# Attention, mixture of experts and gated layer in one kernel: who makes the low parts of the first expert's weights, and when the token list is turned

## The chip, the cores and the metric

The kernel runs on one core of a Trainium2 chip, as a single program with one launch. The metric is the device time in microseconds. The engines are called as in the profile: PE is TensorE, DVE is VectorE, ACT is ScalarE, POOL is GpSimd and SP is SyncE.

## What is computed

Three layers follow one another. Attention with a decay runs over 4 batches of 8 heads, 576 positions, 64 values a head. Its output is read as x with 2304 tokens of 512 values, and goes through a mixture of 8 experts in which each token uses one:

```python
logits = x @ w_gate
e_idx = np.argmax(logits, axis=1)
...
eom = 1.0 / (1.0 + np.exp(-(x @ w_output_gate)))
...
for e in range(E):
    mask = e_idx == e
    ...
    h = np.maximum(x[mask] @ w1[e], 0.0)
    ye = h @ w2[e]
    out[mask] = gate_w[mask, None] * eom[mask, e, None] * ye
```

with w1 of 512 x 1024 and w2 of 1024 x 512 for each expert. The third layer multiplies by w_in (512 x 2048), applies P(h) / (Q(h) + 1e-6) with a cubic P and a quadratic Q, and multiplies by w_out (2048 x 512).

## The kernel before

**Matmuls in two parts.** Operands of the experts and of the third layer are split in two: a high part (ScalarE copies the number into TensorE's float32r form) and a low part (the number less its high part). A product is three matmuls: high by high, high by low, low by high (`mm3`, lines 1164 to 1169, the second of the three on line 1168). `split_unit` (line 1054) does this for a unit of weights: a unit is a quarter of an expert (units 0 and 1 are the halves of w1, 2 and 3 those of w2), 128 x 2048 numbers. Line 1058 makes the high part, in two instructions on ScalarE, and line 1060 the low part, in two instructions on the engine that `on` names. `raw[u]` is the loaded unit, `wu[u]` the split one.

**Slots.** Tokens are sorted by expert into slots of 128. The pipelined loop runs over NPIPE = 22 slots; up to three more, if an expert distribution needs them, are done behind it under `tc.If(spill > 0)`. A small table `esl` describes each slot: whether its expert is a new one, which expert comes next, whether there is one, whether the slot is used. Fourteen small VectorE instructions on 25 partitions make it from `send0` and `pcol` (lines 1016 to 1030), right behind `ids`, the list of tokens of each slot (line 1007). `weights(u, s)` reads `esl`: on ScalarE and VectorE, to split a new expert's unit in slot s under a condition, and on SyncE, to load the next expert's unit into `raw[u]` (line 1110). `spill` is read from `esl` on all engines ahead of the loop (line 1263).

**The order inside a slot is written out by hand** (`tc.manual_schedule`): each engine takes its instructions in the order of the program. For slot s: `gather(s + 3)` (GpSimd, an indirect transfer of 128 rows of x, line 1142); `mm1(s, 0)` with unit 0; `trans_x(s + 1)` (four turns on TensorE, line 1161; then `hi_lo`: the high copy on ScalarE, line 1086, the low part on VectorE, line 1087, into `colA`); `weights(0, s + 1)`; `mm2(s - 1, 0)` and `trans_h(s, 0)` (turns of h, line 1182); `weights(2, s)`; `mm1(s, 1)` with unit 1; `weights(1, s + 1)`; `mm2(s - 1, 1)` and `trans_h(s, 1)`. Slot 0 has no earlier slot: it does `mm1(0,0)`, `trans_x(1)`, `mm1(0,1)`, `trans_h(0,0)`; its `trans_h(0,1)` and first `mm2` stand in slot 1, behind `trans_x(2)`.

**Pieces.** Between these stand four calls `pieces(2)` a slot. Each does two steps of `decode`, which turns w_in and w_out from 64-bit to 32-bit numbers: a transfer issued by GpSimd (line 1201), then ScalarE's absolute value `da` (line 1206) with VectorE's line 1207; line 1209; line 1211; line 1214; ScalarE's high copy (line 1219); VectorE's low part (line 1221).

**What is special in the first slots.** The low part of unit 0 is made ahead of the loop by VectorE, that of unit 1 by VectorE behind `trans_x(0)`, those of units 2 and 3 by GpSimd in slot 0. At slot 0's end stands `slot_tokens()` (line 1126): VectorE copies `ids` to numbers (line 1130), TensorE turns them (line 1132), VectorE copies them back (line 1133) and SyncE stores them as `sid_d`. At slot 1's end stands `dense_rows()` (lines 1112 to 1124), five VectorE instructions that make `yrow`. From slot 2 on, one `gather_word` a slot (line 1148) reads `sid_d` at `yrow`; there are 18.

Of the kernel before, what the change touches and what calls it, by code (L numbers as in the profile page):

```python
# [9 lines left out]
F32 = mybir.dt.float32  # L10
# [3 lines left out]
I32 = mybir.dt.int32  # L14
U32 = mybir.dt.uint32
AF = mybir.ActivationFunctionType
ALU = mybir.AluOpType
AX = mybir.AxisListType
# [3 lines left out]
P = 128  # L22
# [109 lines left out]
def tile_attention_moe_mlp(  # L132
# [16 lines left out]
    nc = tc.nc  # L149
# [3 lines left out]
    NT, DM = out.shape  # L153
    NE, _, FF = w1.shape
# [5 lines left out]
    NSLOT = (NT + NE * (P - 1)) // P  # L160

    NPIPE = min(NSLOT, NT // P + NE // 2)
# [9 lines left out]
    const = ctx.enter_context(tc.tile_pool(name="const", bufs=1))  # L172
# [41 lines left out]
    with ExitStack() as actx, ExitStack() as rctx:  # L214
# [666 lines left out]
        def t_(shape, dt=F32, name=None):  # L881
            return wk.tile(shape, dt, name=name, tag=name, bufs=1)
# [4 lines left out]
        def iota(shape, pattern, base, per_row, name, pool=None):  # L887
            t = pool.tile(shape, F32, name=name) if pool else t_(shape, name=name)
            nc.gpsimd.iota(
                t, pattern=pattern, base=base, channel_multiplier=per_row, allow_small_or_imprecise_dtypes=True  # L890
            )
            return t
# [2 lines left out]
        s1 = t_([P, NSLOT], F16, name="s1")  # L895
        nc.vector.tensor_copy(s1, iota([P, NSLOT], [[1, NSLOT]], 0, 0, "s1f"))
        row = iota([P, P], [[1, P]], 0, 0, "row")
        pcol = iota([P, 1], [[0, 1]], 0, 1, "pcol")

        tokv = iota([P, B, NI], [[S, B], [P, NI]], -(NT // 2), 1, "tokv").rearrange("p b i -> p (b i)")  # L900
        off = t_([P, B, NI], name="off")
# [33 lines left out]
            rows_copy(i)  # L935
        incl, pos3 = t_(SH, name="incl"), t_(SH, name="pos3")
        cnt, nsl = t_([P, NE], name="cnt"), t_([P, NE], name="nsl")
        send0 = t_([P, NE + 1], name="send0")
        nc.gpsimd.memset(send0, 0.0)
        send = send0[:, 1:]  # L940
        base = const.tile([P, NE], F32, name="base")
# [65 lines left out]
        nc.vector.tensor_scalar_add(ids, pid[:, :NSLOT], float(NT // 2))  # L1007

        q = slice(0, NSLOT)
        eq, eo = t_([P, NE + 1], name="eq"), t_([P, NE], name="eo")
        ee, en = t_([P, 1], name="ee"), t_([P, 1], name="en")
        esl = const.tile([P, 4], I32, name="esl")
        chg, usd = t_([P, 1], name="chg"), t_([P, 1], name="usd")
        nc.vector.tensor_scalar(eq[q], send0[q], pcol[q], None, op0=ALU.is_equal)
        nc.vector.tensor_reduce(chg[q], eq[q], AX.X, ALU.max)
        nc.vector.tensor_scalar(eo[q], send[q], pcol[q], None, op0=ALU.is_le)
        nc.vector.tensor_reduce(ee[q], eo[q], AX.X, ALU.add)
        nc.vector.tensor_single_scalar(usd[q], ee[q], NE - 0.5, ALU.is_lt)  # L1020

        nc.vector.scalar_tensor_tensor(eo[q], eo[q], 1.0e6, send[q], ALU.mult, ALU.add)
        nc.vector.tensor_reduce(en[q], eo[q], AX.X, ALU.min)
        nc.vector.tensor_scalar(eo[q], send[q], en[q], None, op0=ALU.is_le)
        nc.vector.tensor_reduce(en[q], eo[q], AX.X, ALU.add)
        nc.vector.tensor_tensor(chg[q], chg[q], usd[q], ALU.mult)
        nc.vector.tensor_copy(esl[q, 0:1], chg[q])
        nc.vector.tensor_scalar_min(esl[q, 1:2], en[q], NE - 1.0)
        nc.vector.scalar_tensor_tensor(esl[q, 2:3], en[q], NE - 0.5, chg[q], ALU.is_lt, ALU.mult)
        nc.vector.tensor_copy(esl[q, 3:4], usd[q])  # L1030


    wu_p = ctx.enter_context(tc.tile_pool(name="wu", bufs=1, reuse_waits="tile"))

    wu = [wu_p.tile([P, 2, KD, 512], F32R, name=f"wu{u}") for u in range(4)]
# [15 lines left out]
            in_offset=bass.IndirectOffsetOnAxis(ap=yrow[:, t : t + 1], axis=0),  # L1051
        )

    def split_unit(u, hi=True, lo=True, on=nc.vector):
        for c in (0, 2):
            w, r = wu[u][:, :, c : c + 2], raw[u][:, c : c + 2]
            if hi:
                nc.scalar.activation(w[:, 0], r, AF.Copy)  # L1058
            if lo:
                on.tensor_tensor(w[:, 1], r, w[:, 0].bitcast(F32), ALU.subtract)  # L1060


    for u in range(4):
        split_unit(u, lo=(u == 0))
    nc.scalar.activation(babs, coef[:, 4:6], AF.Abs)

    with ExitStack() as ectx:
        mk = ectx.enter_context(tc.tile_pool(name="mk", bufs=2, reuse_waits="tile"))
# [7 lines left out]
        def col_of(k):  # L1076
            return tuple(x[:, k] for x in colA)
# [12 lines left out]
        def weights(u, s):  # L1090

            if s:
                if s not in flags:
                    flags[s] = nc.values_load(
                        esl[s : s + 1, 0 : 1], engines=[mybir.EngineType.Activation, mybir.EngineType.DVE],
                        min_val=0, max_val=1,
                    )
                with tc.If(flags[s] > 0):  # L1098
                    split_unit(u)
            if u == order0:  # L1100
                nxt[s] = (
                    nc.sync.value_load(esl[s : s + 1, 1 : 2], min_val=0, max_val=NE - 1),
                    nc.sync.value_load(esl[s : s + 1, 2 : 3], min_val=0, max_val=1),
                )
            e, more = nxt[s]
            if u < 2:
                src = w1[bass.ds(e, 1), :, u * 512 : (u + 1) * 512].rearrange("o (c p) n -> p (o c) n", p=P)
            else:
                src = w2[bass.ds(e, 1), (u - 2) * 512 : (u - 1) * 512, :].rearrange("o (c p) n -> p (o c) n", p=P)
            nc.sync.dma_start(out=raw[u], in_=src, cond=more > 0, bounds_check="skip_entire_dma")  # L1110

        def dense_rows():

            dpad = const.tile([P, NE - 1], F32, name="dpad")
            nc.vector.tensor_tensor(dpad, base[:, 1:], base[:, : NE - 1], ALU.subtract)
            SD = [P, NTILE, NE - 1]
            past = const.tile(SD, F32, name="past")
            nc.vector.tensor_tensor(
                past, dns.unsqueeze(2).to_broadcast(SD), cume[:, 1:NE].unsqueeze(1).to_broadcast(SD), ALU.is_ge
            )  # L1120
            nc.vector.tensor_tensor(past, past, dpad.unsqueeze(1).to_broadcast(SD), ALU.mult)
            drow = const.tile([P, NTILE], F32, name="drow")
            nc.vector.tensor_reduce(drow, past, AX.X, ALU.add)
            nc.vector.tensor_tensor(yrow, drow, dns, ALU.add)

        def slot_tokens():

# [12 lines left out]
        def gather(s):  # L1140
            xg[s] = mk.tile([P, DM], F32, tag="xg", name="xg", bufs=3)
            nc.gpsimd.indirect_dma_start(
                out=xg[s], out_offset=None, in_=x_d[:, :],
                in_offset=bass.IndirectOffsetOnAxis(ap=ids[:, s : s + 1], axis=0),
            )
# [6 lines left out]
        def gather_y(k):  # L1152

            xg[NPIPE + k] = mk.tile([P, DM], F32, tag="xg", name="xg", bufs=3)
            rows_of(k, xg[NPIPE + k])

        def trans_x(s, to):
            pt = ps_x.tile([P, 512], F32, tag="px", name="px")
            t = xg.pop(s)
            for c in range(KD):  # L1160
                nc.tensor.transpose(pt[:, c * P : (c + 1) * P], t[:, c * P : (c + 1) * P], identf)
            xT[s] = hi_lo(pt, to)
# [93 lines left out]
        warm(10)  # L1256
        for s in range(3):
            gather(s)
        trans_x(0, col_of(0))
        weights(0, 0)  # L1260
        split_unit(1, hi=False)
        weights(1, 0)
        spill = nc.values_load(esl[NPIPE : NPIPE + 1, 3 : 4], min_val=0, max_val=1)
        words = deque(range(NTILE))
        for s in range(NPIPE):
            if s + 3 < NPIPE:
                gather(s + 3)
            else:
                gather_y(s + 3 - NPIPE)
            if s >= 2 and words:  # L1270
                t = words.popleft()
                gather_word(dtok[:, t : t + 1], sid_d[:, :], yrow[:, t : t + 1])
            mm1(s, 0)
            if s + 1 < NPIPE:
                trans_x(s + 1, col_of((s + 1) % 2))
                weights(0, s + 1)
            pieces(2)
            if s == 1:
                trans_h(0, 1, col_of(3))
                weights(3, 0)  # L1280
            if s:
                mm2(s - 1, 0)
                trans_h(s, 0, col_of(2))
            if s == 0:
                split_unit(2, hi=False, on=nc.gpsimd)
            weights(2, s)
            pieces(2)
            mm1(s, 1)
            if s + 1 < NPIPE:
                weights(1, s + 1)  # L1290
            pieces(2)

            if s:
                mm2(s - 1, 1)
                trans_h(s, 1, col_of(3))
                weights(3, s)
            else:
                trans_h(0, 0, col_of(2))
                split_unit(3, hi=False, on=nc.gpsimd)
            pieces(2)  # L1300
            if s == 0:
                slot_tokens()
            if s == 1:
                dense_rows()

        gather_y(3)
        for k in range(4):
# [3 lines left out]
        while words:  # L1311
            t = words.popleft()
# [193 lines left out]
```

## Time and profile before

| what | us |
|---|---|
| median of 3 runs | 952.83 (952.47 to 953.22) |
| the profiled execution, its time | 949.95 |
| the profiled execution, its span | 948.1 |
| PE busy | 894.9 |
| DVE busy | 755.4 |
| ACT busy | 623.7 |
| POOL busy | 347.2 |

The busy times are of the whole span, in which attention, experts and third layer follow one another; they are averages over stages with different limits. Times in the rows below count from the span's start. The attention part ends, and the slots begin, at about 240 us.

### The profile page before, as it was taken

The page shows a single profiled execution, that of the slowest core. Times are in us where ns is not written, and L with a number is a line of the kernel's source. Part 1 is how long each engine was busy: PE and PEld are TensorE (multiplying, and loading weights), DVE is VectorE, ACT ScalarE, POOL GpSimd, SP SyncE. Part 2 cuts the span into 40 slices and gives each one's busy share as a digit, 9 for nine tenths or more (in the row PEclk, how much of TensorE's full clock was granted, in tenths as well). Part 3 has the DMA queues.
Part 4 walks back from the last instruction along what each step waited for, and adds up shares of the span by engine and source line. Part 5 has one row for each costly group of instructions (what it writes and reads, how often), then busy time and mean ns, then how long its engine had stood idle before and what let it go on. Part 6 is the DMA issues. An engine that isn't in the chain of part 4 may idle for free. (4 is left out here: it accounts for less than half of the span.)

```text
span 948.1 us, 14923 instructions
## 1 busy us (share of the span) xinstructions
PE 894.9 (94%) x4732; PEld 713.5 (75%) x4733; DVE 755.4 (80%) x1410; ACT 623.7 (66%) x1274; POOL 347.2 (37%) x357
## 2 busy tenths in 40 slices
PE   5999999995589999999999999999999999999996
PEld 5665666563368888888888778889988889988885
DVE  6778888877948668978785499989989878889873
ACT  3787777777036456756653487887777677777664
POOL 7766565624612221312331123243332324223223
PEclk8999999998789999999999999999999999999999
DMA  6754546702455537878864312100100001000001
GB/s 171 168 150 131 157 127 207 210 15 99 138 208 189 194 114 273 298 257 285 287 228 145 135 57 67 34 27 30 34 34 12 23 1 45 24 1 34 1 0 45
DMA packets 50148, 110.26 MB, mean 116 GB/s; under 512 B 8405, under 2 KB 12526, under 8 KB 50062
## 3 DMA queue, kind: packets, MB, share of 16 engines
q1 hardware_dynamic: 39214, 74.09, 25.6%
q0 software_dynamic: 10848, 35.14, 10.8%
q8 instruction: 39, 0.64, 0.3%
q14 instruction: 47, 0.39, 0.1%
HBM read 151.79 MB, written 20.35 MB: 182 GB/s over the span
## 5 line engine op out<-in xcount | busy, mean ns | idle before, releaser
L1405 POOL TENSOR_TENSOR gl<-raw,gh 128x512 fp32r<-128x512 f32 (+1 forms) x80 | 95.4, 1194 | 243.4 <-ACT gh L1404 151.1
L1421 PE MATMUL pa<-wu,gl 128*128 128x512 f32 x288 | 113.0, 392 | 1.1 <-POOL gl L1405 1.1
L1419 PE MATMUL pa<-wu,gh 128*128 128x512 f32 x288 | 113.7, 395 | 0.0
L1420 PE MATMUL pa<-wu,gh 128*128 128x512 f32 x288 | 112.6, 391 | 0.0
L1384 ACT ACTIVATE raw<-ph 128x512 f32<-128x512 f32 (+1 forms) x80 | 44.3, 553 | 79.9 <-PE ph L1376 76.7
L496 ACT ACTIVATE pr<-t,mn 128x384 f32<-128x384 f32 (+3 forms) x128 | 71.1, 557 | 27.6 <-DVE mn L466 25.8
L1087 DVE TENSOR_TENSOR colAl<-px,colAh 128x512 fp32r<-128x512 f32 x70 | 48.0, 687 | 51.4 <-ACTq L1098 28.4
L1060 DVE TENSOR_TENSOR wu<-raw,wu 128x1024 fp32r<-128x1024 f32 x60 | 81.0, 1391 | 7.5 <-ACT wu L1058 7.3
L1387 DVE SCALAR_TENSOR_TENSOR raw<-raw,babs 128x512 f32<-128x512 f32 (+1 forms) x80 | 60.8, 760 | 24.2 <-ACT raw L1385 23.9
L1397 DVE SCALAR_TENSOR_TENSOR raw<-raw,coef,raw 128x512 f32<-128x512 f32 (+1 forms) x80 | 65.9, 824 | 17.6 <-ACT raw L1393 14.5
L1168 PE MATMUL ph<-wu,colAh 128*128 128x512 f32 x176 | 70.7, 402 | 8.2 <-DVE wu L1060 8.2
L1374 PE MATMUL ph<-colAh,wi 128*128 128x512 f32 x192 | 74.9, 390 | 0.8 <-ACTq L1315 0.8
L1375 PE MATMUL ph<-colAl,wi 128*128 128x512 f32 x192 | 74.8, 390 | 0.2 <-DVEq L1315 0.2
L1167 PE MATMUL ph<-wu,colAh 128*128 128x512 f32 x176 | 74.2, 421 | 0.7 <-ACT colAh L1086 0.7
L1376 PE MATMUL ph<-colAh,wi 128*128 128x512 f32 x192 | 74.7, 389 | 0.0
L466 DVE CUSTOM_DVE_ANT_0 t<-s,mask 128x384 f32<-128x384 f32 (+3 forms) x128 | 60.3, 485 | 16.9 <-ACT ot L280 6.9
L1169 PE MATMUL ph<-wu,colAl 128*128 128x512 f32 x176 | 70.7, 402 | 0.0
L1167 PE MATMUL py<-wu,colAh 128*128 128x512 f32 x176 | 70.5, 400 | 0.0
L1169 PE MATMUL py<-wu,colAl 128*128 128x512 f32 x176 | 68.8, 391 | 0.0
L1168 PE MATMUL py<-wu,colAh 128*128 128x512 f32 x176 | 68.7, 390 | 0.0
L614 PE MATMUL po<-pT,v 128*64 128x320 f32 (+4 forms) x448 | 66.4, 380 | 0.4 <-DVE pT L282 0.4
L1086 ACT ACTIVATE colAh<-px 128x512 fp32r<-128x512 f32 x70 | 41.6, 596 | 38.2 <-PE px L1182 25.2
(236 smaller groups left out, 2456.4 us busy)
## 6 DMA issues: line engine op xcount, KB each, us to landing
raw<-in_w_dram SPq DMA_DIRECT2D x92, 1024.0 KB
rk<-in_kT_dram SPq DMA_DIRECT2D x30, 288.0 KB
rq<-in_qT_dram SPq DMA_DIRECT2D x30, 288.0 KB
d<-in_w_in_dram POOLq DMA_DIRECT2D x16, 512.0 KB
d<-in_w_out_dram POOLq DMA_DIRECT2D x16, 512.0 KB
y_d<-ys SPq DMA_DIRECT2D x22, 256.0 KB
v<-in_v_dram SPq DMA_DIRECT2D x16, 256.0 KB
wo_d<-d SPq DMA_DIRECT2D x16, 256.0 KB
```

Of the source, the lines that this page charges most:

```text
L496: nc.scalar.activation(u["pr"][:, :w], u["t"][:, :w], AF.Exp, bias=u["mn"][:, 0:1], scale=-1.0, accum_out=sm[:, i, 2 * hp + h : 2 * hp + h ...
L1060: on.tensor_tensor(w[:, 1], r, w[:, 0].bitcast(F32), ALU.subtract)
L1167: nc.tensor.matmul(ps, hi[:, c, :], w[:, 0, c, :], start=start and c == 0, stop=False)
L1168: nc.tensor.matmul(ps, hi[:, c, :], w[:, 1, c, :], start=False, stop=False)
L1169: nc.tensor.matmul(ps, lo[:, c, :], w[:, 0, c, :], start=False, stop=stop and c == KD - 1)
L1374: nc.tensor.matmul(out_, wh, hi[:, :, c], start=(c == 0), stop=False)
L1375: nc.tensor.matmul(out_, wh, lo[:, :, c], start=False, stop=False)
L1376: nc.tensor.matmul(out_, wl_, hi[:, :, c], start=False, stop=(c == KD - 1))
L1405: nc.gpsimd.tensor_tensor(d["gl"], d["u_"], d["gh"].bitcast(F32), ALU.subtract)
L1419: nc.tensor.matmul(a_, gh[:, sl], wh, start=(m == 0), stop=False)
L1420: nc.tensor.matmul(a_, gh[:, sl], wl_, start=False, stop=False)
L1421: nc.tensor.matmul(a_, gl[:, sl], wh, start=False, stop=(m == MF - 1))
```

## The change

The low parts of all four units of the first expert are made by VectorE: those of units 0 and 1 one after the other behind the first three gathers are issued, those of units 2 and 3 at the places in slot 0 where GpSimd made them. The description of the slots becomes a function, `slot_info()`, with the same fourteen instructions, called behind `trans_x(0)`; its small tiles lie in a buffer of the tag `ys`, and `pcol` and `send0` move to the pool of constants. `slot_tokens()` moves from slot 0's end to slot 1's, ahead of `dense_rows()`; the words are gathered from slot 3 on; `spill` is read at slot 2's end.

```diff
-        pcol = iota([P, 1], [[0, 1]], 0, 1, "pcol")
+        pcol = iota([P, 1], [[0, 1]], 0, 1, "pcol", const)
...
-        send0 = t_([P, NE + 1], name="send0")
+        send0 = const.tile([P, NE + 1], F32, name="send0")
...
-        q = slice(0, NSLOT)
-        eq, eo = t_([P, NE + 1], name="eq"), t_([P, NE], name="eo")
-        ee, en = t_([P, 1], name="ee"), t_([P, 1], name="en")
-        esl = const.tile([P, 4], I32, name="esl")
-        chg, usd = t_([P, 1], name="chg"), t_([P, 1], name="usd")
-        nc.vector.tensor_scalar(eq[q], send0[q], pcol[q], None, op0=ALU.is_equal)
...
-        nc.vector.tensor_copy(esl[q, 3:4], usd[q])
...
-    def split_unit(u, hi=True, lo=True, on=nc.vector):
+    def split_unit(u, hi=True, lo=True):
...
-                on.tensor_tensor(w[:, 1], r, w[:, 0].bitcast(F32), ALU.subtract)
+                nc.vector.tensor_tensor(w[:, 1], r, w[:, 0].bitcast(F32), ALU.subtract)
...
     for u in range(4):
-        split_unit(u, lo=(u == 0))
+        split_unit(u, lo=False)
...
+        esl = const.tile([P, 4], I32, name="esl")
+
+        def slot_info():
+
+
+            q = slice(0, NSLOT)
+            t = mk.tile([P, DM], F32, tag="ys", name="info")
+            eq, eo, rest = t[:, 0 : NE + 1], t[:, 32 : 32 + NE], t[:, 64:68]
+            ee, en, chg, usd = (rest[:, k : k + 1] for k in range(4))
+            nc.vector.tensor_scalar(eq[q], send0[q], pcol[q], None, op0=ALU.is_equal)
+            nc.vector.tensor_reduce(chg[q], eq[q], AX.X, ALU.max)
+            nc.vector.tensor_scalar(eo[q], send[q], pcol[q], None, op0=ALU.is_le)
+            nc.vector.tensor_reduce(ee[q], eo[q], AX.X, ALU.add)
+            nc.vector.tensor_single_scalar(usd[q], ee[q], NE - 0.5, ALU.is_lt)
+
+            nc.vector.scalar_tensor_tensor(eo[q], eo[q], 1.0e6, send[q], ALU.mult, ALU.add)
+            nc.vector.tensor_reduce(en[q], eo[q], AX.X, ALU.min)
+            nc.vector.tensor_scalar(eo[q], send[q], en[q], None, op0=ALU.is_le)
+            nc.vector.tensor_reduce(en[q], eo[q], AX.X, ALU.add)
+            nc.vector.tensor_tensor(chg[q], chg[q], usd[q], ALU.mult)
+            nc.vector.tensor_copy(esl[q, 0:1], chg[q])
+            nc.vector.tensor_scalar_min(esl[q, 1:2], en[q], NE - 1.0)
+            nc.vector.scalar_tensor_tensor(esl[q, 2:3], en[q], NE - 0.5, chg[q], ALU.is_lt, ALU.mult)
+            nc.vector.tensor_copy(esl[q, 3:4], usd[q])
...
         for s in range(3):
             gather(s)
+        split_unit(0, hi=False)
+        split_unit(1, hi=False)
         trans_x(0, col_of(0))
+        slot_info()
         weights(0, 0)
-        split_unit(1, hi=False)
         weights(1, 0)
-        spill = nc.values_load(esl[NPIPE : NPIPE + 1, 3 : 4], min_val=0, max_val=1)
...
-            if s >= 2 and words:
+            if s >= 3 and words:
...
             if s == 0:
-                split_unit(2, hi=False, on=nc.gpsimd)
+                split_unit(2, hi=False)
...
-                split_unit(3, hi=False, on=nc.gpsimd)
+                split_unit(3, hi=False)
             pieces(2)
-            if s == 0:
+            if s == 1:
                 slot_tokens()
-            if s == 1:
                 dense_rows()
+            if s == 2:
+                spill = nc.values_load(esl[NPIPE : NPIPE + 1, 3 : 4], min_val=0, max_val=1)
```

## Rows read from the trace of the kernel before

**Rows 1.** The page's head.

```profile
span 948.1 us, 14923 instructions
```

**Rows 2.** PE's waits from 227 us: total us, times, longest.

```profile
PE ph L1168 <- DVE wu L1060: 8.2, 1, 8.2
PE px L1132 <- DVE ids_t L1130: 3.9, 1, 3.9
```

**Rows 3.** Table by stretches: length, busy PE, PEld, DVE, ACT, POOL; clock, DMA, GB/s.

```profile
257.58:262.54 4.96, 4.95 (x15) 3.76 (x15) 4.19 (x6) 0.34 (x1) 0.56 (x1) 0.62 0.56 169
...
266.44:272.45 6.01, 6.01 (x22) 4.83 (x22) 0.28 (x1) 0.59 (x2) 0.00 (x0) 0.58 0.35 135
...
300.00:400.00 100.00, 100.00 (x491) 82.96 (x490) 75.29 (x101) 60.91 (x93) 24.15 (x27) 1.00 0.62 213
```

**Rows 4.** DVE in order of time: start, us, instruction, idle before it.

```profile
240.04 0.18 DVE L1007 TENSOR_SCALAR ids<-pid 128x25 int32<-128x25 f32 x1 [0.41 <-PE pid L1005]
...
242.13 2.34 DVE L1060 TENSOR_TENSOR wu<-raw,wu 128x1024 fp32r<-128x1024 f32 x2
245.42 0.69 DVE L1087 TENSOR_TENSOR colAl<-px,colAh 128x512 fp32r<-128x512 f32 x1 [0.95 <-ACT colAh L1086]
246.03 12.63 DVE L1060 TENSOR_TENSOR wu<-raw,wu 128x1024 fp32r<-128x1024 f32 x2
258.59 0.68 DVE L1087 TENSOR_TENSOR colAl<-px,colAh 128x512 fp32r<-128x512 f32 x1
259.41 0.43 DVE L1207 TENSOR_SCALAR d<-d 128x512 uint32<-128x512 uint32 x1
...
260.60 0.69 DVE L1211 SCALAR_TENSOR_TENSOR d<-d,d 128x512 uint32<-128x512 uint32 x1
261.40 0.69 DVE L1214 SCALAR_TENSOR_TENSOR d<-da,d 128x512 f32<-128x512 f32 x1
...
266.12 0.17 DVE L1130 CAST ids_t<-ids 128x25 f32<-128x25 int32 x1
```

**Rows 5.** POOL in order of time: two gathers, a decode's transfer, the low parts.

```profile
240.52 1.08 POOL L1142 DMA_INDIRECT xg<-x_d,ids  x1 [4.70 <-DVE eq L1016]
...
245.98 1.16 POOL L1201 DMA_DIRECT2D d<-in_w_in_dram  x2
247.11 9.32 POOL L1060 TENSOR_TENSOR wu<-raw,wu 128x1024 fp32r<-128x1024 f32 x4
...
389.66 1.87 POOL L1142 DMA_INDIRECT xg<-x_d,ids  x1 [0.30 <-PE ph L1169]
```

**Rows 6.** PE's weight loads in order of time: slot 0's turn.

```profile
243.90 0.62 PEld L1161 LDWEIGHTS px<-identf,xg 128*128 128x128 f32 x4 [0.52 <-DMA xg<-x_d,ids]
```

**Rows 7.** PE in order of time.

```profile
248.59 0.60 PE L1161 MATMUL px<-identf,xg 128*128 128x128 f32 x4
...
272.45 0.48 PE L1167 MATMUL py<-wu,colAh 128*128 128x512 f32 x1
...
281.22 0.60 PE L1182 MATMUL px<-identf,h 128*128 128x128 f32 x4
281.57 0.47 PE L1167 MATMUL ph<-wu,colAh 128*128 128x512 f32 x1
```

**Rows 8.** ACT in order of time: the first decode's step.

```profile
252.51 0.66 ACT L1206 ACTIVATE da<-d 128x512 f32<-128x512 f32 x1 [2.64 <-DMA d<-in_w_in_dram]
```

**Rows 9.** DVE in order of time, from slot 1 on.

```profile
282.54 0.69 DVE L1087 TENSOR_TENSOR colAl<-px,colAh 128x512 fp32r<-128x512 f32 x1 [3.15 <-ACTq L1098]
...
284.71 0.16 DVE L1115 TENSOR_TENSOR dpad<-base 128x7 f32<-128x7 f32 x1
...
351.30 0.69 DVE L1214 SCALAR_TENSOR_TENSOR d<-da,d 128x512 f32<-128x512 f32 x1
...
352.74 0.69 DVE L1221 TENSOR_TENSOR wi<-d,wi 128x512 fp32r<-128x512 f32 x1
```

**Rows 10.** Instructions on the tile esl: ns, least, middle, most, first start.

```profile
L1263 PEldq TENSOR_LOAD <-esl x1: 494/494/494, 243.9 to 243.9; - x1
```

More of the change, by code (lines that the diff above doesn't have):

```diff
@@ L1007, in tile_attention_moe_mlp @@
         nc.vector.tensor_scalar_add(ids, pid[:, :NSLOT], float(NT // 2))
-        q = slice(0, NSLOT)
-        eq, eo = t_([P, NE + 1], name="eq"), t_([P, NE], name="eo")
-        ee, en = t_([P, 1], name="ee"), t_([P, 1], name="en")
-        esl = const.tile([P, 4], I32, name="esl")
-        chg, usd = t_([P, 1], name="chg"), t_([P, 1], name="usd")
-        nc.vector.tensor_scalar(eq[q], send0[q], pcol[q], None, op0=ALU.is_equal)
[L1017 to L1029, printed above, removed]
-        nc.vector.tensor_copy(esl[q, 3:4], usd[q])
     wu_p = ctx.enter_context(tc.tile_pool(name="wu", bufs=1, reuse_waits="tile"))
```

## The prediction

> **What bounds the kernel now.** I read the page first: one core, a span of 948.1 us [rows 1]. Then the list of what TensorE waits for behind the attention part: two waits stand out, 8.2 us for `wu` (line 1060) and 3.9 us for `ids_t` (line 1130) [rows 2]. The table by stretches says what they cost. From 300 us on TensorE is busy for 100.00 of 100 us at clock 1.00, so a microsecond that the first slots give back is kept to the end. Behind each of the two waits it runs at a mean clock of 0.62 and 0.58, between its levels of 1.2 and 2.4 GHz [rows 3]. A clock of c over a stretch of length L costs (1 - c) x L against full speed: 0.38 x 4.96 = 1.9 us behind the first wait, 0.42 x 6.01 = 2.5 us behind the second. So the two stalls hold 8.2 + 3.9 + 1.9 + 2.5 = 16.5 us.
>
> Their cause is in VectorE's order of time [rows 4]: the second low part (unit 1, two instructions) takes 12.63 us from 246.03, where the first takes 2.34 us at 242.13. GpSimd runs the low parts of units 2 and 3 just then, 9.32 us for four [rows 5], and VectorE's second instruction starts work when they are over. The wait for `ids_t` is plain order: TensorE's turn of the token list stands ahead of slot 1, and VectorE reaches its copy only at 266.12.
>
> **Removed: the collision.** In the changed order VectorE makes units 0 and 1 right behind `ids` (240.04), 2.34 us each, from about 240.2 to 244.9. The low part of slot 0's columns, at 245.42 before, then finds it free. GpSimd has no low part any more, so nothing holds VectorE, and line 1168 in `mm1(0,1)` finds unit 1 ready: the 8.2 us and the clock lost behind them go. The fourteen small instructions of the slots' description (between 240.04 and 242.13, about 2 us) go behind the columns of slot 0, to about 246.6 to 248.7, when VectorE otherwise waits for slot 1's columns. They cost nothing there; without that cover they would cost their 2 us. SyncE's weight loads, the first readers of `esl`, leave about 5 us later for unit 0, but unit 1's no longer waits for the 12.63 us piece. In VectorE's order of time no low part for a second expert begins ahead of `dense_rows` at 284.71 [rows 9], 35 us on, so I cost that at nothing.
>
> **Added: VectorE against the first gather.** GpSimd's gather of slot 0 took 1.08 us at 240.52 beside small instructions. Now it runs beside split instructions; a gather that did so, at 389.66, took 1.87 us [rows 5]. TensorE's turn of slot 0 waits for that gather's data at 243.90 [rows 6], so a delay of 0 to 0.8 us is passed on; I take 0.5, nearer to the slowed row, since one split instruction is half done when the gather begins. The Trainium skill (SBUF - State Buffer, Who interferes with whom) says that `tensor_tensor` was seen not to stall DMA descriptors, though its second input takes a port that GpSimd reads through. By that the 0.5 us falls away and the time would be 0.5 us lower; the row of 1.87 us differs from it, and the row decides here.
>
> **Moved: units 2 and 3 join VectorE's queue.** Follow both engines, with 0.5 us of shift. Slot 1's columns are turned at 248.59 + 0.5 = 249.1 [rows 7]. The later stretch from 272.45 to 281.22 is 8.77 us: three groups of twelve matmuls and one turn of 0.35 us (281.22 to 281.57), so 2.81 us a group. TensorE then does `mm1(0,1)` from 249.4, a turn, `mm1(1,0)` and two turns, and is ready for `mm2(0,0)` at 249.44 + 2 x 2.81 + 3 x 0.35 = 256.1.
>
> VectorE: slot 1's low columns start 1.32 us behind the turn (as from 281.22 to 282.54 [rows 7, 9]), at 250.4; the decode's first two steps 0.82 us later (258.59 to 259.41) take 1.19 (259.41 to 260.60) [rows 4], to 252.4. That needs the decode's transfer landed by 251.2; before, ScalarE's step on it began at 252.51, released by the transfer [rows 8], while a weight load of 1 MB shared the queues that will now come later. I take it as landed, with 1.2 us as the other bound. Unit 2's low part: 2.34, to 254.8. The next two steps: the second starts 0.80 later, at 255.6; ScalarE's copy and VectorE's last step come 1.44 behind it (351.30 to 352.74 [rows 9]), at 257.0; the low part of slot 0's hidden columns follows at 257.7 and ends at 258.4. The third matmul of `mm2(0,0)` reads it. So the group runs as if started at 257.85: **a wait of 1.7 us, new**.
>
> Unit 3's low part: 258.4 to 260.75. Two decode steps (1.19), slot 2's columns (0.83), two steps (1.49) and the next hidden columns (0.69) end at 264.95. The third matmul of `mm2(0,1)` would be due at 264.4: **0.6 us more**. Its end, and the turn of `h(1,1)`, comes at 257.85 + 8.77 + 0.6 = 267.2.
>
> **The moved token list.** It stands now at slot 1's end, behind that turn and two decode steps. What stood there before was `dense_rows`, whose first instruction began at 284.71, 3.49 us behind the turn at 281.22 [rows 7, 9]. The copy of the list takes that place: 270.7; TensorE's turn comes 0.32 later (266.12 to 266.44 [rows 3, 4]), at 271.0, and `mm1(2,0)` at once. So the wait is not removed but moved: from the end of the turn before it (267.8) about **3.2 us, against 3.9**. `dense_rows`, some 1.2 us behind it, lies beside slot 2's matmuls. Its words are gathered from slot 3 on, eighteen by slot 20; POOL has room.
>
> After that idle the clock is lost again, I think: 3.9 us were followed by 2.5 us of loss, 8.2 by 1.9 [rows 2, 3]. The 3.9 us came behind a stretch at 0.62, the moved stall comes behind some 10 us at full speed; so I take the smaller, 1.9, with 0 and 2.5 as bounds. The read of `spill` on all engines at slot 2's end took 0.494 us of TensorE's sequencer [rows 10], beside a wait; there it stands behind matmuls already queued: 0, at most 0.5.
>
> **The sum.** `mm1(2,0)` started at 281.57; now at 271.05: 10.5 us. Less 1.9 of clock: **8.6 us**. The other way: 16.5 less (0.5 + 1.7 + 0.6 + 3.2 + 1.9) gives 8.6. The profiled execution took 949.95 us (span 948.1), 2.9 below the median; 949.95 - 8.6 = 941.35, and on the median 952.83 - 8.6 = **944.2 us**. Best bounds: + 0.5 (gather) + 1.9 (clock) gives 11.0, 941.8. Worst: - 0.3 - 1.2 - 0.6 - 0.5 gives 6.0, 946.8.
>
> **Rivals.** (1) *The clock holds* through the moved stall: 952.83 - 10.5 = 942.3. For it: the stall is shorter than 3.9 and lies in full-speed work. Against: both stalls of before lost it.
> (2) *The gather is held by all four split instructions*, as VectorE was held by GpSimd's four [rows 4, 5]: its description of 1.08 us would start at 244.9 instead of 240.52, 4.4 us late against the 0.5 taken, so 3.9 us less: 948.1. Against: the slowed row shows 0.8.
> (3) *Slower: VectorE waits in order for the decode's transfer.* The low parts of units 2 and 3 stood on GpSimd, free of it; now they are queued behind the first decode step. Two weight loads leave together around 250 and may share the queues with it. Each microsecond of landing past 251.2 costs one; it decides at 251.2 + 8.6 = 259.8, from where the kernel is slower. Against: with one weight load beside it the data was there by 252.51 [rows 8], 6.5 us behind its issue at 245.98 [rows 5]. If a second load doubles that, it lands at 259: 952.83 - 0.8 = 952.0.
> (4) *The change doesn't do what it says*: VectorE's low parts stay slow for another reason than GpSimd, and 8.2 us return elsewhere: 952.83 - 8.6 + 8.2 = 952.4. Against: the two at 242.13, beside no low part on GpSimd, took 2.34 [rows 4].
>
> **Chances.** Forecast with its bounds, 941.8 to 946.8: 0.60. Rival 1: 0.22. Rival 2: 0.08. Rival 3: 0.07, of it 0.04 past its deciding point. Rival 4: 0.03. The first two hold 0.82 between 941.5 and 947.2 with the spread of the runs (0.4), which is the range; rivals 2 to 4 are left out. A measurement of this kernel can tell about 0.2% (1.9 us) from no change. Faster: 0.60 + 0.22 + 0.08 and part of rival 3, 0.92; same: 0.04; slower: 0.04.
>
> **What would show it.** Right: the wait of line 1168 for `wu` is gone; all split instructions on VectorE are near 1.2 us, none on GpSimd; new short waits of `mm2(0,0)` and `mm2(0,1)` for `colAl`; a wait of 3 to 4 us for `ids_t` just ahead of `mm1(2,0)`, at about 271; half clock behind it. Wrong: no wait for `ids_t`, or full clock behind it (rival 1); the first gather over 2 us (rival 2); the first decode step on VectorE past 253 (rival 3). The prediction fails most likely in the length of VectorE's chain up to `mm2(0,0)`, or in the clock.

## The result and the profile after

The changed kernel takes 943.46 us (median of 4 runs, 942.01 to 945.64) against 952.65 us (4 runs, 951.17 to 953.22) for the kernel before in the same comparison: a ratio of 0.9908, with a 95% interval of 0.9884 to 0.9932. That is 9.2 us faster, where 8.6 was forecast. The profiled execution took 944.24 us.

The page of the changed kernel: its head, and the one group of low parts. Before, some of these ran on POOL [rows 5]; now all 64 are on DVE, at a mean of 1220 ns (the span answers to [rows 1]).

```profile
span 942.5 us, 14908 instructions
...
L1037 DVE TENSOR_TENSOR wu<-raw,wu 128x1024 fp32r<-128x1024 f32 x64 | 75.3, 1220 | 7.0 <-ACT wu L1035 6.6
```

The changed kernel's list of PE's waits from 227 us, the rows that answer to [rows 2]:

```profile
PE px L1134 <- DVE ids_t L1132: 3.2, 1, 3.2
PE px L1163 <- DMA xg<-x_d,ids: 1.2, 1, 1.2
...
PE py L1169 <- ACT colAh L1063: 0.9, 1, 0.9
...
PE py L1171 <- DVE colAl L1064: 0.2, 1, 0.2
```

The 8.2 us for `wu` are gone. The wait for `ids_t` is still there, at 3.2 us instead of 3.9. What is new is short: 0.9 and 0.2 us in `mm2(0,0)`, and 1.2 us for the first gather.

DVE of the changed kernel in order of time (start, us, instruction, idle before it), against [rows 4]:

```profile
239.92 0.18 DVE L1007 TENSOR_SCALAR ids<-pid 128x25 int32<-128x25 f32 x1 [0.41 <-PE pid L1005]
240.12 4.63 DVE L1037 TENSOR_TENSOR wu<-raw,wu 128x1024 fp32r<-128x1024 f32 x4
245.95 0.69 DVE L1064 TENSOR_TENSOR colAl<-px,colAh 128x512 fp32r<-128x512 f32 x1 [1.20 <-ACT colAh L1063]
246.56 0.40 DVE L1112 TENSOR_SCALAR info<-send,pcol 25x9 f32<-25x9 f32 x1
...
248.64 0.13 DVE L1126 CAST esl<-info 25x1 int32<-25x1 f32 x1
251.74 0.69 DVE L1064 TENSOR_TENSOR colAl<-px,colAh 128x512 fp32r<-128x512 f32 x1 [2.96 <-ACT colAh L1063]
252.73 0.43 DVE L1209 TENSOR_SCALAR d<-d 128x512 uint32<-128x512 uint32 x1 [0.30 <-DVEq L1075]
...
253.80 2.35 DVE L1037 TENSOR_TENSOR wu<-raw,wu 128x1024 fp32r<-128x1024 f32 x2
...
258.91 0.68 DVE L1064 TENSOR_TENSOR colAl<-px,colAh 128x512 fp32r<-128x512 f32 x1
259.51 2.35 DVE L1037 TENSOR_TENSOR wu<-raw,wu 128x1024 fp32r<-128x1024 f32 x2
261.78 0.42 DVE L1209 TENSOR_SCALAR d<-d 128x512 uint32<-128x512 uint32 x1
...
265.01 1.28 DVE L1064 TENSOR_TENSOR colAl<-px,colAh 128x512 fp32r<-128x512 f32 x2
...
271.64 0.17 DVE L1132 CAST ids_t<-ids 128x25 f32<-128x25 int32 x1
```

Four low parts in 4.63 us, then two pairs of 2.35: no piece of 12.63 us is left. The description's fourteen instructions end at 248.77, 2.96 us before VectorE has anything else to do. The first decode step at 252.73 was not released by its transfer.

POOL of the changed kernel in order of time, the first two gathers, against [rows 5]:

```profile
240.39 1.91 POOL L1144 DMA_INDIRECT xg<-x_d,ids  x1 [4.70 <-DVE ids L1007]
242.61 1.86 POOL L1144 DMA_INDIRECT xg<-x_d,ids  x1 [0.30 <-issue]
```

PE of the changed kernel in order of time, against [rows 6, 7]:

```profile
244.63 0.65 PE L1163 MATMUL px<-identf,xg 128*128 128x128 f32 x4 [1.16 <-DMA xg<-x_d,ids]
245.97 0.73 PE L1169 MATMUL ph<-wu,colAh 128*128 128x512 f32 x1 [0.69 <-ACT colAh L1063]
...
250.42 0.60 PE L1163 MATMUL px<-identf,xg 128*128 128x128 f32 x4
250.78 0.48 PE L1169 MATMUL ph<-wu,colAh 128*128 128x512 f32 x1
...
253.61 0.60 PE L1184 MATMUL px<-identf,h 128*128 128x128 f32 x4
...
257.27 0.60 PE L1184 MATMUL px<-identf,h 128*128 128x128 f32 x4
258.75 0.50 PE L1169 MATMUL py<-wu,colAh 128*128 128x512 f32 x1 [0.88 <-ACT colAh L1063]
...
262.07 0.60 PE L1184 MATMUL px<-identf,h 128*128 128x128 f32 x4
...
271.96 0.27 PE L1134 MATMUL px<-identf,ids_t 128*25 128x128 f32 x1 [3.21 <-DVE ids_t L1132]
271.98 0.47 PE L1169 MATMUL ph<-wu,colAh 128*128 128x512 f32 x1
...
276.77 0.48 PE L1169 MATMUL py<-wu,colAh 128*128 128x512 f32 x1
```

PE of the kernel before in order of time, the two rows that [rows 7] leave out:

```profile
245.44 0.50 PE L1167 MATMUL ph<-wu,colAh 128*128 128x512 f32 x1 [0.69 <-ACT colAh L1086]
...
284.76 0.48 PE L1167 MATMUL py<-wu,colAh 128*128 128x512 f32 x1
```

The table by stretches of the changed kernel, columns as in [rows 3]:

```profile
245.97:250.42 4.45, 4.45 (x12) 3.36 (x13) 2.57 (x15) 0.00 (x0) 2.10 (x3) 0.62 0.80 242
...
271.98:276.77 4.79, 4.79 (x17) 3.79 (x18) 1.31 (x6) 0.47 (x1) 0.10 (x1) 0.65 0.35 112
300.00:400.00 100.00, 100.00 (x486) 82.38 (x485) 76.74 (x103) 60.96 (x93) 25.65 (x28) 1.00 0.67 227
```

Two places at a lower mean clock remain. One is behind the moved list. The other was not forecast: `mm1(0,0)`, the first group, takes 4.45 us from 245.97 to 250.42, where it took 3.15 before (245.44 to the turn at 248.59 [rows 7]). That is 1.3 us.

By position in the two profiles, `mm1(2,0)` starts at 271.98 instead of 281.57 [rows 7], 9.6 us earlier, and the group behind it, `mm2(1,0)`, at 276.77 instead of 284.76, 8.0 earlier. The spans differ by only 5.6. So this pair of executions gives back 2.4 us behind slot 2. Of it, 1.0 lies in waits: 0.6 us in a later slot and 0.8 in the third layer that the trace of before does not have, against 0.4 in one that only it has. The other 1.4 is the spacing of the slots' matmuls, 0.2300 us from start to start on the mean between 285 and 400 us against 0.2285, or 12.37 us a slot against 12.30, over some twenty slots. The medians, over four runs each, differ by 9.2, so the pair seems to understate the gain: before's profiled 949.95 us lies 2.7 below its median here and after's 944.24 lies 0.8 above.

### The profile page after: what moved, and what is told of

The parts are those of the page before. It is cut to its first block, busy times and chain, and to the rows that moved or that the text cites. A ratio compares the mean times of both kernels' runs of the same rounds, so it can differ in the third digit from the quotient of the medians.

```text
span 942.5 us, 14908 instructions
## 1 busy us (share of the span) xinstructions
PE 896.6 (95%) x4733; PEld 713.4 (76%) x4733; DVE 749.4 (80%) x1414; ACT 623.9 (66%) x1274; POOL 339.3 (36%) x353
## 5 line engine op out<-in xcount | busy, mean ns | idle before, releaser
L1037 DVE TENSOR_TENSOR wu<-raw,wu 128x1024 fp32r<-128x1024 f32 x64 | 75.3, 1220 | 7.0 <-ACT wu L1035 6.6
```

The lines of the kernel that those rows point to most:

```text
L1037: nc.vector.tensor_tensor(w[:, 1], r, w[:, 0].bitcast(F32), ALU.subtract)
```

## Experiments

Theory: the gain is the collision's stall and the clock behind it, the moved list still stalls, and the three edits (low parts, description, list) need each other. Rivals: the list's move alone bought the gain; it makes no difference which engine makes the low parts of units 2 and 3, once units 0 and 1 are done early; the description's place counts for nothing.

**Only the low parts of units 2 and 3, in the kernel before.**

```diff
-                split_unit(2, hi=False, on=nc.gpsimd)
+                split_unit(2, hi=False)
...
-                split_unit(3, hi=False, on=nc.gpsimd)
+                split_unit(3, hi=False)
```

> One part alone: the kernel before, with only the engine of units 2 and 3 changed from GpSimd to VectorE; the token list stays at slot 0's end, the slots' description ahead of unit 0. Theory (the collision is gone, but the low parts of units 2 and 3 then stand ahead of the token list's copy in VectorE's order, so TensorE waits there instead): the wait of 8.2 us for wu goes, the wait for ids_t grows from 3.9 to about 9 us, and the kernel is 4 to 5 us faster than before, about half of the change's 9.2. Rival (the collision alone makes the gain, the place of the token list is worth nothing): 9 us faster.

Measured: 949.18 us (9 runs), ratio 0.9961 (0.9947 to 0.9975), 2.6 us faster where 4 to 5 were expected. The longest of its PE waits behind the attention part:

```profile
PE px L1132 <- DVE ids_t L1130: 12.4, 1, 12.4
```

and its DVE in order of time:

```profile
246.12 2.35 DVE L1060 TENSOR_TENSOR wu<-raw,wu 128x1024 fp32r<-128x1024 f32 x2
...
254.46 0.43 DVE L1207 TENSOR_SCALAR d<-d 128x512 uint32<-128x512 uint32 x1 [3.79 <-DMA d<-in_w_in_dram]
```

Unit 1's low part takes 2.35 us from 246.12, where it took 12.63 from 246.03 [rows 4]: GpSimd's low parts were what held it. But the stall goes to `ids_t`, which grows from 3.9 to 12.4 us, 3.4 more than expected. The second row says why: VectorE stands 3.79 us before its first decode step, waiting for the transfer, and all that is queued behind it is late. Here the description is early and unit 1's low part no longer late, so the first weight load leaves at 244.42 and the second at 248.59, while that transfer, issued at 246.06, is still under way; before, the second left only at 258.79. The transfer's data are there some 2 us later than in [rows 8]. This is rival 3's mechanism, at work in another kernel than the one it was written for; that the loads cause the delay is read from the times.

**Only the list's move, in the kernel before.**

```diff
-            if s >= 2 and words:
+            if s >= 3 and words:
...
-            if s == 0:
+            if s == 1:
                 slot_tokens()
-            if s == 1:
                 dense_rows()
```

> The other part alone: the kernel before, with only the token list's turn and store moved to slot 1's end and the words gathered from slot 3 on. Theory (the stall for ids_t is moved, not removed; the collision of unit 1 with GpSimd stays): the wait of 8.2 us stays, the wait for ids_t is 3 to 4 us in its new place, the time is 0 to 2 us lower than before, 951 to 953. Rival (the stall in slot 0 and its half clock are what the move saves): 4 to 6 us faster.

Measured: 950.73 us (12 runs), ratio 0.9989 (0.9972 to 1.0005), no difference that can be told. The two longest of its PE waits behind the attention part:

```profile
PE ph L1168 <- DVE wu L1060: 8.2, 1, 8.2
PE px L1132 <- DVE ids_t L1130: 3.2, 1, 3.2
```

The list's move alone only turns 3.9 into 3.2. Apart, the two edits give 2.6 and 1.0 us against the kernel before as it was measured beside them (951.78), together with the description's move some 9. The description's move alone in the kernel before, and the changed kernel with the list left at slot 0's end, were not run.

**The list turned early: its copy and turn ahead of the low parts, the store behind slot 0's turn.** In the changed kernel `slot_tokens()` gets a `yield` behind its transpose:

```diff
+        tokens = slot_tokens()
+        next(tokens)
         split_unit(0, hi=False)
         split_unit(1, hi=False)
         trans_x(0, col_of(0))
+        next(tokens, None)
...
             if s == 1:
-                slot_tokens()
                 dense_rows()
```

> The changed kernel, with the token list turned earlier: VectorE copies it ahead of the low part of unit 0, TensorE turns it while it waits for the first gather, VectorE copies it back behind the columns of slot 0. Theory (the 3.2 us for ids_t and the half clock behind it, 1.4 us more by the matmuls' spacing, are a loss that is left): the wait is gone, no half clock at slot 2's start, 4 to 5 us faster than the changed kernel, 938.5 to 939.5. Rival (VectorE's chain through slot 1 is what TensorE waits for, and the wait turns up at the next colAl): 0 to 1 us faster than the changed kernel.

Measured: 938.53 us (936.37 to 939.54, 5 runs), ratio 0.9849 (0.9828 to 0.9870), whose interval lies below that of the changed kernel: about 5 us faster than it. Its PE waits from 242 to 300 us are these and two of 0.7 and 0.2:

```profile
PE py L1170 <- ACT colAh L1063: 0.9, 1, 0.9
...
PE px L1164 <- DMA xg<-x_d,ids: 0.6, 1, 0.6
```

and its PE in order of time:

```profile
246.00 0.42 PE L1134 MATMUL px<-identf,ids_t 128*25 128x128 f32 x1
...
248.36 0.50 PE L1170 MATMUL ph<-wu,colAh 128*128 128x512 f32 x1 [0.69 <-ACT colAh L1063]
...
251.50 0.60 PE L1164 MATMUL px<-identf,xg 128*128 128x128 f32 x4
```

No wait for `ids_t`, a granted clock of 1.00 from 248.36 to 285 us, and `mm1(0,0)` at 3.14 us. Three items of the changed kernel are gone: 3.2 for the list, 1.6 behind it, 1.3 of `mm1(0,0)`, 6.1 in all. From the start of `ids` to that of `mm2(1,0)` this trace is 6.0 us shorter than that of the changed kernel. The medians show 4.9, about what the first two make.

**The changed kernel with units 2 and 3 back on GpSimd.**

```diff
-                split_unit(2, hi=False)
+                split_unit(2, hi=False, on=nc.gpsimd)
...
-                split_unit(3, hi=False)
+                split_unit(3, hi=False, on=nc.gpsimd)
```

> One part undone: the changed kernel with the low parts of units 2 and 3 back on GpSimd; unit 1 still stands ahead of them on VectorE. Theory (GpSimd's four instructions now hold VectorE's next instruction with two inputs in SBUF, the decode's second step, to about 257, instead of unit 1's low part): mm2(0,0) waits 2 to 3 us longer for its low columns than in the changed kernel, later slots are as there, and the time is 0 to 2 us above it. Rival (VectorE's work is what counts: 4.7 us less of it in front of mm2(0,0) and mm2(0,1)): 2 to 3 us faster than the changed kernel.

Measured: 950.84 us (12 runs), ratio 0.9991 (0.9973 to 1.0008): the whole gain is gone, and the expectation failed. The longest of its PE waits behind the attention part (that of 3.2 us for `ids_t` is there as well):

```profile
PE ph L1169 <- ACTq L1075: 6.8, 1, 6.8
```

its DVE in order of time:

```profile
252.16 10.54 DVE L1112 TENSOR_SCALAR info<-send,pcol 25x9 f32<-25x9 f32 x1
```

and its POOL in order of time:

```profile
252.15 1.16 POOL L1203 DMA_DIRECT2D d<-in_w_in_dram  x2
253.28 9.38 POOL L1037 TENSOR_TENSOR wu<-raw,wu 128x1024 fp32r<-128x1024 f32 x4
```

I had thought that with units 0 and 1 done early nothing was left on VectorE to be held. It was the next in line that was held: the first instruction of the description, on 25 x 9 elements, takes 10.54 us instead of 0.40, until GpSimd's last low part is over at 262.66. `esl` is late, so ScalarE's and VectorE's reads of the flag are, and slot 1's first group waits 6.8 us on ScalarE's queue. (In this execution the attention part ended some 5 us later than in the others; only distances are read from it.)

**The description ahead of the low parts.**

```diff
+        slot_info()
         split_unit(0, hi=False)
         split_unit(1, hi=False)
         trans_x(0, col_of(0))
-        slot_info()
```

> One part undone: the changed kernel with the slots' description ahead of the low parts of units 0 and 1 again. Theory (behind them the description holds back the first two weight loads, and so lets the decode's transfer pass, which VectorE waits for with units 2 and 3 queued behind): the loads leave about 5 us earlier, VectorE's first decode step begins at about 254.5 from an ids at 240, as in the run with only units 2 and 3 changed, instead of 252.7; unit 1 ends at about 247 and its columns follow 1 us later; 1.5 to 3 us slower than the changed kernel. Rival (the description's place only decides what lies beside the first gather: beside small instructions it takes 1.1 us instead of 1.9): 0.7 us faster, and up to 2 us more if mm1(0,0) then runs at full clock.

Measured: 945.11 us (6 runs), ratio 0.9934 (0.9908 to 0.9960); its interval overlaps that of the changed kernel, so its loss (1.7 us by the medians, 2.5 by the ratios) is in the expected direction, not more. Its DVE and its PE waits:

```profile
254.76 0.43 DVE L1209 TENSOR_SCALAR d<-d 128x512 uint32<-128x512 uint32 x1 [1.45 <-DMA d<-in_w_in_dram]
```

```profile
PE py L1169 <- ACT colAh L1063: 2.0, 1, 2.0
```

The trace fits the mechanism: with `esl` early, the first weight load leaves at 245.99, ahead of the decode's transfer (issued at 247.93), and the second at 248.26; in the changed kernel both leave behind it, from 250.50 on. VectorE waits for that transfer again, 1.45 us, and `mm2(0,0)` waits 2.0 instead of 0.9. `mm1(0,0)` also waits 0.8 us for slot 0's low columns, since the fourteen instructions now stand ahead of them. Against that the first gather took only 1.09 us and `mm1(0,0)` lost no clock, so that from `ids` to `mm2(1,0)` only 0.4 us is lost.

**Three more warm matmuls ahead of slot 0.**

```diff
-        warm(10)
+        warm(13)
```

> The changed kernel with 13 instead of 10 idle matmuls ahead of slot 0's turn, so that TensorE works until the gathered rows are there, which come 0.7 us later than before. Theory (the 1.2 us without work in front of the turn kept the clock at its lower level for most of mm1(0,0), 1.6 us lost): mm1(0,0) at 2.4 GHz, 1 to 2 us faster than the changed kernel. Rival (when the clock rises has nothing to do with that gap, and differs from run to run): no change within 0.5 us.

Measured: 941.78 us (6 runs), ratio 0.9898 (0.9872 to 0.9925). Its PE in order of time:

```profile
249.31 0.50 PE L1169 MATMUL ph<-wu,colAh 128*128 128x512 f32 x1 [0.69 <-ACT colAh L1063]
...
252.46 0.60 PE L1163 MATMUL px<-identf,xg 128*128 128x128 f32 x4
```

`mm1(0,0)` is at full speed again, 3.15 us instead of 4.45, and the 1.2 us of idle time ahead of the turn are gone. But the three matmuls also hold the turn back, which comes 5.3 us behind the start of `ids` instead of 4.7, so that up to `mm2(1,0)` 0.7 us is gained and not 1.3. The medians differ by 1.7 us, about the expected amount, but the intervals overlap: not settled in the time. Nor is the idle time shown to be the cause, because the next kernels have a trace in which a longer pause cost nothing.

**`send0` 32 bytes wider, which shifts the buffers behind it; alone, and with the early list.**

```diff
-        send0 = const.tile([P, NE + 1], F32, name="send0")
+        send0 = const.tile([P, NE + 9], F32, name="send0")[:, : NE + 1]
```

> The changed kernel with send0 32 bytes a partition wider (nothing reads the added part). In the slots the changed kernel's matmuls start 0.2300 us apart, before 0.2285, at the same granted clock; in the third layer both have the same pace. By their addresses in the two programs wu0 lay at 52640 before (32 above a multiple of 128) and lies at 52736 in the changed kernel (a multiple of 128), since pcol and send0 moved to the constants; here it lies at 52768, 32 above again. Theory (the place of wu and colA in SBUF sets that pace): 0.2285 us again, and some 1060 matmuls x 1.5 ns = 1.6 us faster than the changed kernel, about 942. Rival (the pace has another cause, such as the moved read of spill): 0.2300, no change.

> The kernel with the early token list (938.5 us), with send0 32 bytes wider too. Theory of the pace: the two add, 1.6 us faster, 937. Rival: 938.5.

Measured: 943.22 us (6 runs), ratio 0.9918 (0.9891 to 0.9946), and with the early list 939.78 us (6 runs), ratio 0.9866 (0.9838 to 0.9895). The slots' spacing fell from 0.2300 us to 0.2292 and 0.2291, about half of the way to the 0.2285 of before, and the times stayed within their intervals. The spacing goes with the program, not with the execution: it is 0.2284 to 0.2286 in the three traces of kernels with the constants of before, and 0.2299 to 0.2301 in the five with those of the changed kernel. The list's move does not set it, since one of the three has that move. So the place of the buffers may have a part in the spacing, but no gain in time is shown. What sets the rest stays open.

PE of the kernel with both, in order of time:

```profile
247.37 0.66 PE L1164 MATMUL px<-identf,xg 128*128 128x128 f32 x4 [1.51 <-DMA xg<-x_d,ids]
248.71 0.50 PE L1170 MATMUL ph<-wu,colAh 128*128 128x512 f32 x1 [0.69 <-ACT colAh L1063]
...
251.85 0.60 PE L1164 MATMUL px<-identf,xg 128*128 128x128 f32 x4
...
260.83 0.50 PE L1170 MATMUL py<-wu,colAh 128*128 128x512 f32 x1 [1.52 <-ACT colAh L1063]
...
265.71 0.60 PE L1185 MATMUL px<-identf,h 128*128 128x128 f32 x4
```

Here TensorE stood idle for 1.51 us ahead of the turn, longer than in the changed kernel, and `mm1(0,0)` still ran at full speed, 3.14 us. The clock was lost behind the next wait instead: `mm2(0,0)` takes 4.88 us at a mean clock of 0.65, where the changed kernel takes 3.32.

**All runs side by side.** The distance from the start of `ids` to that of `mm2(1,0)` in each profiled execution leaves out how late the attention part ended; the ratio is of all runs to the kernel before.

| kernel | `ids` to `mm2(1,0)`, us | ratio |
|---|---|---|
| before | 44.7 | 1 |
| low parts of units 2 and 3 only | 42.5 | 0.9961 |
| list's move only | 43.9 | 0.9989 |
| changed | 36.9 | 0.9908 |
| changed, units 2 and 3 on GpSimd | 44.0 | 0.9991 |
| changed, description first | 37.3 | 0.9934 |
| changed, thirteen warm matmuls | 36.1 | 0.9898 |
| changed, wider `send0` | 36.9 | 0.9918 |
| changed, list early | 30.8 | 0.9849 |
| changed, list early, wider `send0` | 32.8 | 0.9866 |

## Why the prediction was right

**The collision.** Right in cause and size. The wait of 8.2 us is gone and the low parts run at 1.2 us each. Two experiments bear it out from both sides: taking GpSimd's low parts away frees the held instruction in the kernel before, and giving them back in the changed kernel takes the whole gain. Rival 4 falls.

**The gather.** 1.91 us beside the low parts instead of 1.08, its turn at 244.63 instead of 243.90, `mm1(0,0)` 0.53 us later; predicted 0.5. Rival 2 (four instructions' worth) falls: the gather was held for the rest of one low part, the one already under way. The Trainium skill (SBUF — State Buffer, Who interferes with whom) says that `tensor_tensor` was seen not to stall DMA descriptors; the row of 1.91 us differs from that, as the row of 1.87 did.

**A term that was left out.** Nothing in the sum priced the clock of `mm1(0,0)`: 1.3 us. In the profile of the changed kernel the granted clock rose to 1.00 at 242.65 us, while the warm matmuls ran. TensorE then stood idle for 1.16 us until the gathered rows came and for 0.69 us behind the turn, and from 246.1 to 249.3 the clock was 0.50. I had passed on the delay of the gather, but not asked what the pause does. With `send0` wider the trace shows the same loss (4.44 us for `mm1(0,0)`), with thirteen warm matmuls it is gone. That the pause alone does it is not shown: 1.51 us cost nothing in the kernel with the early list and the wider `send0`. So this term's cause, and whether every execution of the changed kernel pays it, stay open.

**The waits in slot 0.** VectorE's chain was sized well: from slot 1's low columns to those of slot 0's hidden part it takes 258.91 - 251.74 = 7.2 us, predicted 7.3. The profile shows only 0.88 + 0.16 = 1.0 us of idle time in `mm2(0,0)`, but the forecast of 1.7 counts otherwise, by where the whole group lies. Its turn at 262.07 puts its end, less the 2.83 us of a group (250.78 to 253.61), at a start of 259.24; TensorE could have started it 0.35 behind the turn at 257.27, at 257.62. So the wait is 1.6 us. It is not shortened by the clock of `mm1(0,0)`, which delays VectorE's chain as well: with thirteen warm matmuls, where that clock is not lost, the idle times are 0.92 and 0.17. `mm2(0,1)` does not wait at all (predicted 0.6): from one hidden part's low columns to the next VectorE takes 265.01 - 258.91 = 6.1 us, where the prediction comes to 6.6. It added up full lengths, and the instructions start closer together than that (259.51 to 261.78 is 2.27, for a pair of 2.35).

**The moved list.** Predicted 3.2 us at 271.0; measured 3.21 at 271.96. The prediction's reading, that the wait is moved and not removed, is borne out by the list's move alone and by the early list, which removes it. Rival 1 falls as well: behind the stall the clock was lost, 271.98 to 276.77 is 4.79 us against 3.19 for the same group before (281.57 to 284.76), so 1.6, predicted 1.9. The same 4.8 us stand in all six traces whose list is turned at that place.

**The decode's transfer.** Taken as landed by 251.2; the step began at 252.73 with no wait for it. Rival 3 falls for this kernel. But it was met in two other kernels, and what holds it off here is the description's place, which I had costed only by the cover of its 2 us: where the description stays early, VectorE waits 3.79 us (in the kernel before) or 1.45 (in the changed one) for this transfer. That later weight loads keep the queues free was named in the prediction as a reason; its price is seen only in these runs.

**The sum.** By position 9.6 us at `mm1(2,0)` (predicted 10.5) and 8.0 with the clock (predicted 8.6); by the medians 9.2. The clock of `mm1(0,0)`, 1.3 us, was missing from the sum; the 0.6 us of `mm2(0,1)` and 0.3 us of the clock behind the list did not come; some 0.2 us lies in small differences of turns and spacing. That leaves the 0.6 us by which 8.0 falls short of 8.6. That these errors have opposite signs is luck, and so is part of the closeness of 944.2 to 943.46: within the pair of profiles the forecast (941.35) missed by 2.9 us, 0.6 by these steps and 2.4 by the waits and the spacing behind slot 2, which no step priced.

## What to carry to other kernels

Look for a VectorE instruction many times its usual length and for what GpSimd does until its end; here it did not help to do VectorE's work earlier while GpSimd's series remained, since the next instruction in line was held. When a stall is removed, follow the queue to what is late next: here the low parts' move alone made the wait for the list grow to 12.4 us, and the description left early made VectorE wait for the decode's transfer. A small turn that sits in front of a busy TensorE is worth placing where TensorE still waits anyway, since a stall of 3 us also costs clock behind it.

## What the runs showed of the hardware

A VectorE instruction that was begun some 1.1 us ahead of a series of four low parts on GpSimd ended only behind the series. In the kernel before, the first of unit 1's two took from 246.03 to 257.53, and GpSimd's series ended at 256.43; with units 2 and 3 back on GpSimd, an instruction on 25 x 9 elements took 10.54 us instead of 0.40. Both began just behind the start of GpSimd's transfer issue, but the issue alone is not what held them: with units 2 and 3 on VectorE, a low part begun at the same place beside it took its usual 1.2 us. The Trainium skill (SBUF — State Buffer, Who interferes with whom) says that the two engines share a pair of ports and that the one that comes second is blocked for the length of the other's instruction. Here VectorE was not let in between one instruction of GpSimd's and the next.

The other way round the hold was short. A gather that began while a low part was running on VectorE ended 0.8 to 1.0 us behind that one instruction, and a following low part did not hold it. The first gather of the changed kernel ended at 242.31, with the low part under way over at 241.35; the one at 475.68 took 1.33 us, with the low part over at 476.13. In the kernel before, the gather at 243.19 took 0.97 us: the low part under way was over 0.15 us later.

TensorE fell to the lower level of its clock after 3.2 us of idle time behind work at full speed (1.6 us lost); in the changed kernel it fell some 1.4 us after work had begun again. Shorter pauses differ from trace to trace: idle times of 1.16 and 0.69 us around the turn were followed by 1.3 us of loss in the changed kernel, 1.51 and 0.69 us by none with the early list and the wider `send0`.

The spacing of the slots' matmuls, with the same shapes, was 0.2285, 0.2292 or 0.2300 us by kernel; its cause is not settled.
